# Group 3 by the DMA crossbar, in the one buffer that the later groups share

## The chip, the cores and the metric

The kernel runs on one core of a Trainium2 chip. The metric is device time in microseconds, the median of the runs of one kernel. The core has TensorE (PE, matmuls and their weight loads), VectorE (DVE), ScalarE (ACT) and GpSimd (POOL), and SyncE (SP), which here only issues DMAs. POOL issues the loads that convert from float32 to bfloat16. SP issues the stores of the result and the transposing DMAs through the crossbar. Each engine works through its own instructions in program order; semaphores hold one back until its inputs are there and its output buffer is free.

## The reference, cut to what matters

A sliding-window attention with four sink tokens feeds a SwiGLU block with three weight matrices.

```python
batch, n_heads, seq, head_dim = (4, 8, 768, 64)
n_sink, window = (4, 128)
scores = scale * np.matmul(q, k.transpose(0, 1, 3, 2))
keep = is_sink | in_window                 # 128 keys back, and keys 0 to 3
a = softmax(np.where(keep, scores, -1e9))
attn_out = np.matmul(a, v)                 # (4, 8, 768, 64)

x = attn_out.transpose(0, 2, 1, 3).reshape(3072, 512)
g, val = x @ w_gate, x @ w_val             # 512 -> 1536
out = (g * sigmoid(g) * val) @ w_out       # 1536 -> 512, float32
```

## The kernel before

The 3072 tokens of the attention are cut into 12 groups of 256, three to a batch. Group g is worked on in steps: its keys and queries are loaded with tokens in the partitions (`load_nat`), transposed so that the head's elements lie in the partitions, multiplied to scores (`step_S`), exponentiated, multiplied with the values (`step_PV`), normalised, and turned into columns of `xT` for the SwiGLU block (`step_X`). The SwiGLU block takes 8 blocks of tokens; `gate` does two projections, `down` the last one. The attention steps of later groups are woven between the `gate` and `down` steps of earlier blocks, so that TensorE always has matmuls at hand.

There are two ways to transpose keys and queries. `step_TN` lets TensorE do it into PSUM, and ACT or DVE copy the result out. `xbar` lets the DMA do it, from SBUF to SBUF, with four instructions from SP.

```python
rowp = pool("rowp", 3)     # three buffers, at first for staging, later for two groups
natp = pool("natp", 1)     # one buffer
...
def load_nat(g):
    b, c = divmod(g, GC)
    x = (natp if g > 3 else rowp).tile(
        [P, 2, 2, DM], BF16, tag="nat" if g > 3 else "rows", name="nat")
    for i, src in ((0, k), (1, q)):
        for j in range(2):
            t0 = c * 256 + j * P
            nc.gpsimd.dma_start(
                x[:, i, j].rearrange("p (h d) -> p h d", d=D),
                src[b, :, t0:t0 + P].rearrange("h p d -> p h d"))
    nats[g] = x

def load_v(g):
    b, c = divmod(g, GC)
    va = vpool.tile([P, 2, H, VS], BF16, tag=f"va{g}", name="va")   # a buffer per group
    nc.vector.memset(va[:, :, :, D:D + 1], 1.0)
    for j in range(2):
        ...
        nc.gpsimd.dma_start(va[:, j, :, 0:D], ...)
...
def step_TN(g, i, j, evict="av"):
    ...
    for p in range(NP2):
        nc.tensor.transpose(pt[:, p], nats[g][:, i, j, p * P:(p + 1) * P], ident)
    ...
    if evict[i] == "a":
        nc.scalar.copy(out=dst, in_=pt)
    else:
        nc.vector.tensor_copy(out=dst, in_=pt)

def xbar(g):
    ...
    for j in range(2):
        for i in range(2):
            t0 = c * 256 + j * P
            nc.sync.dma_start_transpose(
                (kTs, qTs)[i][b][:, :, t0:t0 + P], nats[g][:, i, j])
...
def step_X(g, j, evict="v"):
    ...
    if g not in PEX:                      # PEX = (0, 1, 2, 4)
        def sp():
            nc.sync.dma_start_transpose(xTs[tb][:, :, off:off + P], xns[g, j])
        later.append(sp)
        return
    ...
...
def down(tb, ts, attn, last=False):
    ...
        nc.scalar.activation(ot, po, AF.Copy, scale=0.5)
        nc.sync.dma_start(out[r0:r0 + P, lo:hi], ot)
...
flush()
load_nat(3)
load_v(3)
...
def NV(g):
    return L(A(load_nat, g), A(load_v, g))

# slot number -> attention steps woven into that gate or down step;
# slots 0 to 17 are gates of blocks 0 to 2, slots 18 to 23 their down steps
weave(us, slots(
    ...
    (11, [NV(4)]), ((14, 14, 15, 15), TN(3, "aa")),
    (15, [A(xbar, 4)]), (15, [NV(5)]), (19, [A(xbar, 5)]), (19, [NV(6)]),
    (23, [A(xbar, 6)]), (23, [NV(7)]),
    ((17, 18), Ss(3)), (18, [A(step_ks, 1)]), (18, [A(step_vsb, 1)]),
    ((19, 19, 19, 20), PVs(3)), (20, Xs(3)),
    ((19, 20), Ss(4)), (19, [K(4)]),
    ((21, 21, 22, 22), PVs(4)), (22, Xs(4))))
...
# block 3 (groups 3 and 4): gates, then down steps, with groups 5 and 6 woven in
weave(gates(3) + downs(3), slots(
    (2, [A(xbar, 7)]), (2, [NV(8)]),
    (5, [A(step_ks, 2), A(step_vsb, 2)]), *pair(5, 6),
    (15, [A(xbar, 8)]), (15, [NV(9)])))
```

A tile is given its buffer when it is asked for, and the first DMA into a buffer waits until all uses of the tile that held it before are done. So the load of group 5 into the single `nat` buffer waits for the four transposes of group 4 that read it, and so on to group 11.

Of the kernel before, what the change touches and what calls it, by code (L numbers as in the profile page):

```python
# [8 lines left out]
BF16 = mybir.dt.bfloat16  # L9
# [5 lines left out]
def kernel(  # L15
# [13 lines left out]
    P = 128  # L29
# [3 lines left out]
    DM = moe_w_gate.shape[0]  # L33
# [7 lines left out]
    NG = B * GC  # L41
# [11 lines left out]
    def pool(name, bufs, psum=False):  # L53
        if psum:
            return ctx.enter_context(
                tc.tile_pool(name=name, bufs=bufs, space=bass.MemoryType.PSUM))
        return ctx.enter_context(tc.tile_pool(name=name, bufs=bufs))
# [3 lines left out]
    rowp = pool("rowp", 3)  # L61
    natp = pool("natp", 1)
# [15 lines left out]
    def bank(shape, dtype, name):  # L78
        return psum.tile(shape, dtype, tag="b", name=name)


    rows, nats, vas = {}, {}, {}
# [20 lines left out]

    def load_nat(g):
        b, c = divmod(g, GC)
        x = (natp if g > 3 else rowp).tile(
            [P, 2, 2, DM], BF16, tag="nat" if g > 3 else "rows", name="nat")
        for i, src in ((0, k), (1, q)):
            for j in range(2):
                t0 = c * 256 + j * P  # L110
# [7 lines that stand above are left out]
        va = vpool.tile([P, 2, H, VS], BF16, tag=f"va{g}", name="va")  # L118
# [4 lines that stand above are left out]
                va[:, j, :, 0:D], v[b, :, t0:t0 + P].rearrange("h p d -> p h d"))  # L123
        vas[g] = va
# [71 lines left out]
    load_gate(2)  # L196
    nc.gpsimd.tensor_copy(out=vcf[64:128], in_=vcf[0:64])
    load_nat(2)
    load_gate(3)
    load_v(2)  # L200
# [18 lines left out]
    def new_T(b):  # L219
        if b not in kTs:  # L220
            kTs[b] = kqtp.tile([P, NP2, S], BF16, tag="kT", name="kT")
            qTs[b] = kqtp.tile([P, NP2, S], BF16, tag="qT", name="qT")
# [17 lines left out]
        else:  # L240
            nc.vector.tensor_copy(out=dst, in_=pt)

    def step_TN(g, i, j, evict="av"):

        b, c = divmod(g, GC)
        new_T(b)
        pt = bank([P, NP2, P], BF16, "pn")
        for p in range(NP2):
            nc.tensor.transpose(pt[:, p], nats[g][:, i, j, p * P:(p + 1) * P], ident)  # L249
        t0 = c * 256 + j * P  # L250
        dst = (kTs, qTs)[i][b][:, :, t0:t0 + P]
        if evict[i] == "a":
            nc.scalar.copy(out=dst, in_=pt)
        else:
            nc.vector.tensor_copy(out=dst, in_=pt)
# [213 lines left out]
    def gates(tb):  # L469
        return [(gate, tb, f) for f in range(0, DFC, 512 // SIZES[tb])]  # L470
# [4 lines left out]
    def A(fn, *a):  # L475
        return lambda: fn(*a)

    def TN(g, evict="av"):
        return [A(step_TN, g, i, j, evict) for j in range(2) for i in range(2)]

    def Ss(g):
        return [A(step_S, g, p2) for p2 in range(2)]
# [116 lines left out]
    later[:0] = masks1  # L599
    flush()  # L600
    load_nat(3)
    load_v(3)

    g0, g1, g2 = gates(0), gates(1), gates(2)
    us = [g0[0], g0[1], g0[2], g1[0], g1[1],
# [3 lines left out]
    def L(*fs):  # L609
        def f():  # L610
            for x in fs:
                x()
        return f

    def NV(g):
        return L(A(load_nat, g), A(load_v, g))

    weave(us, slots(
        (0, [K(1)]), (1, PVs(1)[:2] + [A(step_PV, 1, 0, 1, "a"), A(step_PV, 1, 1, 1, "a"), flush]),
        (2, [A(step_X, 1, 0, "a"), A(step_X, 1, 1, "a")]),  # L620
        ((4, 4, 5, 5), TN(2)), ((6, 7), Ss(2)), (6, [K(2)]),
        ((8, 8), PVs(2)[:2]), (9, [A(step_PV, 2, 0, 1, "a"), A(step_PV, 2, 1, 1, "a")]),
        ((10, 11), [A(step_X, 2, 0, "a"), A(step_X, 2, 1, "a")]),
        (11, [NV(4)]), ((14, 14, 15, 15), TN(3, "aa")),
        (15, [A(xbar, 4)]), (15, [NV(5)]), (19, [A(xbar, 5)]), (19, [NV(6)]),
        (23, [A(xbar, 6)]), (23, [NV(7)]),
        ((17, 18), Ss(3)), (18, [A(step_ks, 1)]), (18, [A(step_vsb, 1)]),
        ((19, 19, 19, 20), PVs(3)), (20, Xs(3)),
# [58 lines left out]
```

The softmax here doesn't subtract the row's maximum and nothing guards it: scores larger than these inputs give would overflow.

## Time and profile before

| | |
|---|---|
| median of 3 runs | 240.88 us (240.53 to 240.91) |
| span of the profiled run | 239.5 us |
| mean granted TensorE clock | 0.998 |
| PE busy | 232.2 us, 97% of the span |
| DVE busy | 158.6 us, 66% |
| ACT busy | 114.6 us, 48% |
| POOL busy (almost all of it issuing loads) | 73.2 us, 31% |
| share of the chain that ended last: PE | 84% |
| bytes read from HBM | 28.34 MB |
| written to HBM | 6.29 MB |

Busy time of the DMA-issuing instructions is the time to issue; a transfer lands later, and the profile gives the time from issue to landing for POOL's loads. The end of SP's transposing DMAs shows only in who waits for them. A row of the timeline has the start, the time covered, the engine, the line of the kernel, the operation with output and inputs, the count, and in brackets the idle time just before it and what ended it. "SPq" is SyncE's queue.

### The profile page before, as it was taken

How to read it: one execution, taken by the hardware profiler on the slowest of the kernel's cores; microseconds unless marked ns; L12 is line 12 of the kernel's file. 1: busy time of each engine (PE TensorE's matmuls, PEld its weight loads, DVE VectorE, ACT ScalarE, POOL GpSimd, SP SyncE). 2: the span in 40 equal slices, each digit the busy share in tenths (PEclk: the TensorE clock that was granted, in tenths of full speed). 3: DMA queues.
4: the chain of work that ended last, by engine and by line, in shares of the span. 5: the costliest groups of instructions: out<-in, count | busy, mean ns of one | idle time of the engine just before them, and what ended most of it. 6: DMA issues, size and time to landing. Idle time of an engine off the chain costs nothing.

```text
span 239.5 us, 4998 instructions
## 1 busy us (share of the span) xinstructions
PE 232.2 (97%) x1952; PEld 133.4 (56%) x1952; DVE 158.6 (66%) x336; ACT 114.6 (48%) x237; POOL 73.2 (31%) x94
## 2 busy tenths in 40 slices
PE   8998999999999999999999999999999999999994
PEld 5766978895454444444444454445454445488443
DVE  4799679678742898950798981588961598877000
ACT  3896385556552845512745611556611662332112
POOL 8985874712508043260080700071000000000000
PEclk9999999999999999999999999999999999999999
DMA  8999999993999999799699984699504200200122
GB/s 138 172 179 175 183 200 204 154 127 69 151 174 167 147 133 140 104 118 211 114 101 134 118 46 136 118 112 145 66 0 145 77 0 3 44 0 3 65 112 88
DMA packets 107591, 27.36 MB, mean 114 GB/s; under 512 B 94640, under 2 KB 104624, under 8 KB 107568
## 3 DMA queue, kind: packets, MB, share of 16 engines
q0 software_dynamic: 76640, 13.90, 75.7%
q1 hardware_dynamic: 30400, 12.89, 27.9%
q8 instruction: 15, 0.25, 0.4%
q10 hardware_dynamic: 528, 0.26, 0.4%
q14 instruction: 8, 0.07, 0.1%
HBM read 28.34 MB, written 6.29 MB: 145 GB/s over the span
## 4 chain that ended last, share of the span: by engine, by line
PE 84%; POOL 5%; DMA 4%; DVE 3%; issue 1%; ACT 1%; POOLq 0%; DVEq 0%; ACTq 0%
PE pd L458 26%; PE pv L427 24%; PE pg L427 24%; DMA wv<-in_moe_w_val_dram 4%; PE s L296 4%; PE o L359 4%; POOL va L122 1%; POOL rows L100 1%; DVE u L440 1%; PE pn L249 1%; POOL x L183 1%; POOL wg L133 1%; DVE ht L441 1%; POOL wv L133 1%; PE pk L324 1%
## 5 line engine op out<-in xcount | busy, mean ns | idle before, releaser
L427 PE MATMUL pv<-xT,wv 128*128 128x256 bf16 (+1 forms) x384 | 74.3, 326 | 1.1 <-DMA wv<-in_moe_w_val_dram 0.7
L427 PE MATMUL pg<-xT,wg 128*128 128x256 bf16 (+1 forms) x384 | 74.2, 326 | 0.9 <-DVE u L440 0.5
L434 ACT ACTIVATE th<-pg 128x512 f32<-128x512 f32 x72 | 43.5, 604 | 62.6 <-PE pg L427 62.1
L440 DVE SCALAR_TENSOR_TENSOR u<-th,pg 128x512 bf16<-128x512 f32 x72 | 49.2, 683 | 35.7 <-ACT th L434 35.7
L458 PE MATMUL pd<-wo,ht 128*128 128x512 bf16 (+1 forms) x300 | 66.2, 371 | 0.0
L441 DVE TENSOR_TENSOR ht<-u,pv 128x512 bf16<-128x512 bf16 x72 | 49.5, 688 | 11.5 <-PE pv L427 5.1
L427 PEld LDWEIGHTS <-wg 128*128 128x128 bf16 x384 | 37.4, 98 | 26.7 <-issue 1.3
L427 PEld LDWEIGHTS <-wv 128*128 128x128 bf16 x384 | 34.3, 98 | 20.5 <-issue 1.6
L303 ACT ACTIVATE e<-s 128x512 bf16<-128x512 f32 (+1 forms) x88 | 42.7, 582 | 3.9 <-PE s L296 3.9
L458 PEld LDWEIGHTS <-ht 128*128 128x128 bf16 x300 | 28.1, 98 | 28.7 <-issue 0.5
L111 POOL DMA_DIRECT2D nat<-in_k_dram x20 | 17.6, 884 | 79.6 <-DMA qT<-nat 68.5
L462 ACT ACTIVATE ot<-pd 128x512 f32<-128x512 f32 (+1 forms) x25 | 14.6, 583 | 48.4 <-PE pd L458 48.4
L308 DVE TENSOR_TENSOR e<-e,mask 128x1024 bf16<-128x1024 bf16 (+1 forms) x44 | 26.9, 649 | 3.6 <-ACT e L303 3.6
L122 POOL DMA_DIRECT2D va<-in_v_dram x24 | 21.5, 918 | 5.2 <-DMA wo<-in_moe_w_out_dram 2.5
L359 PEld LDWEIGHTS <-e 128*128 128x128 bf16 x352 | 15.4, 98 | 8.3 <-issue 0.3
L373 DVE TENSOR_TENSOR xn<-o,rcp 128x256 bf16<-128x256 f32 x44 | 18.7, 425 | 1.5
L111 POOL DMA_DIRECT2D nat<-in_q_dram x20 | 17.7, 897 | 1.8 <-DMA wg<-in_moe_w_gate_dram 1.2
L359 PE MATMUL o<-va,e 128*128 128x65 bf16 x352 | 17.5, 193 | 0.2 <-DMA va<-in_v_dram 0.2
L296 PE MATMUL s<-qT,kT 64*128 64x128 bf16 (+1 forms) x240 | 13.1, 237 | 0.0
L367 DVE RECIPROCAL rcp<-o 128x4 f32<-128x4 f32 x48 | 8.2, 175 | 5.6 <-PE o L359 5.4
L296 PEld LDWEIGHTS <-kT 64*128 64x128 bf16 x240 | 7.7, 94 | 7.3 <-issue 6.8
L133 POOL DMA_DIRECT2D wv<-in_moe_w_val_dram x6 | 4.8, 803 | 0.5 <-DMA wv<-in_moe_w_val_dram 0.5
(66 smaller groups left out, 84.0 us busy)
## 6 DMA issues: line engine op xcount, KB each, us to landing
out_dram<-ot SPq DMA_DIRECT2D x23, 256.0 KB
va<-in_v_dram POOLq DMA_DIRECT2D x24, 128.0 KB, 6.2
nat<-in_k_dram POOLq DMA_DIRECT2D x20, 128.0 KB, 4.0
nat<-in_q_dram POOLq DMA_DIRECT2D x20, 128.0 KB, 5.6
wg<-in_moe_w_gate_dram POOLq DMA_DIRECT2D x6, 256.0 KB, 8.0
wv<-in_moe_w_val_dram POOLq DMA_DIRECT2D x6, 256.0 KB, 8.5
wo<-in_moe_w_out_dram POOLq DMA_DIRECT2D x4, 384.0 KB, 11.1
st<-in_q_dram ACTq DMA_DIRECT2D x1, 256.0 KB
```

The source lines that it names most:

```text
L111: nc.gpsimd.dma_start(x[:, i, j].rearrange("p (h d) -> p h d", d=D), src[b, :, t0:t0 + P].rearrange("h p d -> p h d"))
L122: nc.gpsimd.dma_start(va[:, j, :, 0:D], v[b, :, t0:t0 + P].rearrange("h p d -> p h d"))
L296: nc.tensor.matmul(pss[2 * pp + h][:, col:col + n], kTs[b][r, p, kk:kk + P], qTs[b][r, p, qq:qq + n], start=True, stop=True)
L303: nc.scalar.activation(e_t[g][:, h0 + h, lo:512], pss[2 * pp + h][:, lo:512], AF.Exp, scale=scale)
L308: nc.vector.tensor_tensor(e, e, m[:, :, lo:512].broadcast_to([P, 2, 512 - lo]), op=ALU.mult)
L359: nc.tensor.matmul(o, l, r, start=(c == 0 and i == 0), stop=(i == len(mms) - 1), skip_group_check=True)
L373: nc.vector.tensor_tensor(xn, po[:, :, 0:D], rcp.broadcast_to([P, 4, D]), op=ALU.mult)
L427: nc.tensor.matmul(ps[:, i * n:(i + 1) * n], ws[fi][:, c, fo * P:(fo + 1) * P], x[:, c], start=(c == 0), stop=(c == DMC - 1))
L434: nc.scalar.activation(th, pg, AF.Tanh, scale=0.5)
L440: nc.vector.scalar_tensor_tensor(u, th, 1.0, pg, op0=ALU.add, op1=ALU.mult)
L441: nc.vector.tensor_tensor(hts[tb][:, f:f + two].rearrange("p a n -> p (a n)"), u, pv, op=ALU.mult)
L458: nc.tensor.matmul(po, hts[tb][:, f, ts * P:(ts + 1) * P], wos[f // n][:, f % n, lo:hi], start=(f == 0), stop=(f == DFC - 1))
```

## The change

Group 3's keys and queries are no longer transposed by TensorE out of a `rows` buffer; they go into the single `nat` buffer and are transposed by the crossbar, as those of the groups after it are. As the load of group 4's keys and queries then has to wait until group 3's have left that buffer, and would hold up all that POOL issues behind it, the values are moved ahead of it: group 4's values are loaded right after group 3's, and then group g + 1's values follow group g's keys and queries. It is meant to free TensorE of 16 transposes and ScalarE of 4 copies. The parameter that said which engine copies is dropped, as only group 2 uses `step_TN` now, with its default.

```diff
     def load_nat(g):
         b, c = divmod(g, GC)
-        x = (natp if g > 3 else rowp).tile(
-            [P, 2, 2, DM], BF16, tag="nat" if g > 3 else "rows", name="nat")
+        x = (natp if g > 2 else rowp).tile(
+            [P, 2, 2, DM], BF16, tag="nat" if g > 2 else "rows", name="nat")
...
-    def step_TN(g, i, j, evict="av"):
+    def step_TN(g, i, j):
...
-        if evict[i] == "a":
+        if i == 0:
             nc.scalar.copy(out=dst, in_=pt)
         else:
             nc.vector.tensor_copy(out=dst, in_=pt)
...
     flush()
     load_nat(3)
     load_v(3)
+    load_v(4)
...
     def NV(g):
-        return L(A(load_nat, g), A(load_v, g))
+        return L(A(load_nat, g), A(load_v, g + 1)) if g + 1 < NG else A(load_nat, g)
...
-        (11, [NV(4)]), ((14, 14, 15, 15), TN(3, "aa")),
+        (11, [A(xbar, 3)]), (11, [NV(4)]),
         (15, [A(xbar, 4)]), (15, [NV(5)]), (19, [A(xbar, 5)]), (19, [NV(6)]),
         (23, [A(xbar, 6)]), (23, [NV(7)]),
```

More of the change, by code (lines that the diff above doesn't have):

```diff
@@ L476, in A, with TN @@
         return lambda: fn(*a)
-    def TN(g, evict="av"):
-        return [A(step_TN, g, i, j, evict) for j in range(2) for i in range(2)]
+    def TN(g):
+        return [A(step_TN, g, i, j) for j in range(2) for i in range(2)]
     def Ss(g):
```

## The prediction, made before the run

> **What bounds the kernel now.** I read the page's busy row first, then the chain of work that ended last, then the list of who waited for whom, then the timelines of SyncE's queue, of GpSimd and of TensorE where the change lies (42 to 80 us), and the times from issue to landing of single loads. Busy row and chain:
>
> ```profile
> PE 232.2 (97%) x1952; PEld 133.4 (56%) x1952; DVE 158.6 (66%) x336; ACT 114.6 (48%) x237; POOL 73.2 (31%) x94
> ...
> PE 84%; POOL 5%; DMA 4%; DVE 3%; issue 1%; ACT 1%; POOLq 0%; DVEq 0%; ACTq 0%
> ```
>
> TensorE bounds it: 97% busy, and after about 23 us the chain hardly leaves it. Taking work from TensorE shortens the time by that work; any wait that TensorE gets lengthens it by that wait. What stands in the way is shown by the wait list:
>
> ```profile
> POOL nat L111 <- DMA qT<-nat: 68.5, 6, 20.7
> ```
>
> GpSimd waits 68.5 us in six waits for transposes of queries to leave the single buffer before it may load the next group. That costs nothing today, but it is a chain of its own (load, transpose, release, load), and the change puts one more group at its head. Its pace, from the timelines of SyncE and GpSimd:
>
> ```profile
> 50.24 1.29 SPq L263 DMA_TRANSPOSE kT<-nat  x1
> 51.98 1.76 SPq L263 DMA_TRANSPOSE qT<-nat  x1
> 53.83 1.22 SPq L263 DMA_TRANSPOSE kT<-nat  x1
> 55.14 1.22 SPq L263 DMA_TRANSPOSE qT<-nat  x1
> ...
> 67.37 2.00 SPq L263 DMA_TRANSPOSE qT<-nat  x1
> 69.46 0.53 SPq L463 DMA_DIRECT2D out_dram<-ot  x1
> 70.09 2.53 SPq L392 DMA_TRANSPOSE xT<-xn  x2
> ```
>
> ```profile
> 42.19 0.87 POOL L111 DMA_DIRECT2D nat<-in_k_dram  x1 [0.60 <-DMA wo<-in_moe_w_out_dram]
> ...
> 58.12 1.75 POOL L111 DMA_DIRECT2D nat<-in_k_dram  x2 [9.40 <-DMA qT<-nat]
> ...
> 71.79 1.76 POOL L111 DMA_DIRECT2D nat<-in_k_dram  x2 [8.42 <-DMA qT<-nat]
> ```
>
> Group 4 is loaded from 42.19 us, with no wait for a buffer, since it is the first in it. Its last transpose is issued at 55.14, and the buffer is free at 58.12 (2.98 us later). Group 5 takes the buffer from 58.12 to 71.79 (13.7 us). The page's digits of DMA share stand at 9 up to about 54 us: weights, then groups 3 and 4, drain one behind the other. TensorE at the three places that matter:
>
> ```profile
> 48.84 0.61 PE L249 MATMUL pn<-ident,nat 128*128 128x128 bf16 x8
> 49.29 1.04 PE L427 MATMUL pv<-xT,wv 128*128 128x256 bf16 x8
> ...
> 62.05 0.62 PE L296 MATMUL s<-qT,kT 64*128 64x128 bf16 x12
> ...
> 76.60 1.03 PE L427 MATMUL pg<-xT,wg 128*128 128x512 bf16 x4
> ```
>
> The first pair is half of group 3's transposes by TensorE, the third row group 4's first scores, the last row the first matmul of block 3. None of them waits for a DMA today: group 4's transposed queries are there 4 us before 62.05.
>
> **What the Trainium skill says.** "Perfetto Trace Analysis", section "DMA Instruction — HWDGE (DVE, Sync)", says that the profiled window of such a DMA is its issue and not the movement of its data. The trace agrees: the transpose issued at 55.14 ends its window at 56.36, and the buffer is free only at 58.12. So I count from issue to release. "DMA: Bandwidth & Descriptors", section "Issuing engines are not separate DMA queues", says that DMAs of all issuing engines run on the same 16 DMA engines and interleave. The trace agrees with sharing: the transpose that was issued while loads were still landing took 1.76 us instead of 1.22, and group 6, loaded beside three stores of 256 KB, held the buffer 15.1 us (71.79 to 86.91) against 11.7 us of group 9 (119.45 to 131.19). "TensorE: Matmul & The Clock Gate", section "What's actually happening", says that an idle window of about 3.4 us halves TensorE's clock. No run here shows it, the granted clock is 0.998; it matters to the upper end of the range.
>
> **The change, part by part.**
> Removed from TensorE: two times 8 transposes. From 48.84 to 49.29 and from 51.04 to 51.48 they take 0.45 and 0.44 us, together 0.89 us, on the path that sets the end. So -0.9 us.
> Removed from ACT: four copies of 580 to 606 ns, 2.4 us. ACT is 48% busy and idles before its next activation for want of TensorE (62.1 us in the wait list), so this is worth 0.
> Added: four transposing DMAs on SyncE, which has nothing else to issue from about 5.3 to 50 us. Worth 0 by themselves.
> Moved: group 4's values stand before its keys and queries. They take the places in the load queue that those had (two loads, issued at about 42.2 and 44.1). The values are no longer held up by the buffer, which prevents a worse result but wins nothing here: no value was late before (the only wait of a matmul for a value is one of 0.2 us).
> Moved, and this is the point: group 4's keys and queries now wait for the buffer. Step by step:
> 1. Group 3's load. Its four pieces are issued at 32.72, 33.79, 35.10 and 36.44, as before, and land 12.0, 11.9, 11.6 and 11.1 us later, at 44.7, 45.7, 46.7 and 47.5.
> 2. Its transposes go out in order keys, queries, keys, queries: 44.7, then 46.7 when the first queries land, then one after the other. With one prolonged issue of 1.76 beside the loads still draining: 48.5, then 49.8. Released 2.98 us after that: 52.8. The scores of group 3 are wanted at 55.07 - 0.9 = 54.2; that just holds.
> 3. Group 4's load begins at 52.8 instead of 42.19. From there to the release I take group 9's 11.7 us and not group 5's 13.7, because no store can get in front of or between these transposes in SyncE's queue. So group 4 is there at 64.5.
> 4. TensorE arrives at its scores at 62.05 - 0.9 = 61.15. It waits 64.5 - 61.15 = 3.35 us. All later work shifts by 3.35 - 0.9 = +2.45 us.
> 5. Group 5: loaded at 64.5, between 11.7 and 13.7 us, say 12.5: free at 77.0, its last transpose issued some 3.3 us before that, at 73.7. Behind it in SyncE's queue stand one store (0.5 us) and group 3's two columns of xT (1.3 us apart): 75.4 and 76.7 instead of 70.09 and 71.4. They land about 2.8 us after issue, at 79.5. TensorE wants them for block 3 at 76.60 + 2.45 = 79.05. A second wait of about 0.45 us.
> 6. Group 5's scores are wanted at 77.56 + 2.9 = 80.5 and are there at 77.0. Group 6 is loaded at 77.0, beside three stores as before, so 15.1 us: there at 92.1, wanted at 90.51 + 2.9 = 93.4. It holds by 1.3 us. From group 7 on the trace has slack: 7 is released at about 100 and wanted after 113. The delay is absorbed and no more is added.
> Sum: -0.9 + 3.35 + 0.45 = +2.9 us; 240.9 + 2.9 = 243.8 us.
>
> **The rivals.**
> First, the load chain holds and only TensorE's 0.9 us show: 240.0 us. For it: group 4's queries were ready 4 us before they were wanted, and group 3's buffer could be released faster than I think. Against it: the load starts 10.6 us later (42.19 to 52.8), it lands quicker by some 4.5 us as the queue is empty by then (8.0 us from issue to landing of its first piece before, 3.3 us for group 5), and of the remaining 6 us the slack covers only 4, less 0.9 as TensorE comes sooner.
> Second, the chain runs slower than I think: each cycle 13.7 us or more. Then group 4 comes at 66.5, group 5 at 80.2, the columns of xT at 82.7 against 81.0 wanted, and group 6 at 95.3 against 97. That is about +6.2 us, 247 us. For it: groups 5 and 6 took 13.7 and 15.1. Against it: stores contended there, and a late chain meets fewer of them.
> Third, the idle stretch of over 3 us makes TensorE's clock drop and adds one or two microseconds. Against it: a stall of 3.35 us hardly contains a whole window.
> A fourth, that ACT bounds something and its copies count, is refuted by its 62.1 us of waiting for TensorE.
>
> **Range and chances.** The centre is 243.8 us. The first rival bounds it below (240.0), but it needs both cycles to be 3 us shorter than any that the trace shows, so the low end is 241.8. The second rival gives 247.0 as the high end. The 2% limit above is 245.7: reached if the first two cycles together take about 2 us longer than I assume, 0.18. Faster by over 2% would need 4.8 us from a change that takes 0.9 us off TensorE: 0.02. Within 2%: 0.80.
>
> **What would show it.** In the changed kernel's timeline SyncE should issue group 3's transposes from 44.7 to about 49.8, GpSimd should start group 4's keys near 52.8 after a wait for "qT<-nat", and TensorE should show idle time of 3 to 3.5 us before the scores of group 4 with DMA qT or kT as releaser; that releaser should appear in the wait list of PE or its weight loads, where it is absent now. The two xT transposes should be issued near 75 to 77 us, with a small wait of the first pg matmul of block 3. After block 3's start no new wait should show. The prediction is wrong if group 4's first scores start before 62 us, if group 3's scores wait for their own transposes by more than a microsecond, or if a wait for DMA appears at group 6 or later.

## The result, and the profile after

The change makes the kernel slower: 246.92 us median against 240.91 us, a ratio of 1.0251 (95% interval 1.0217 to 1.0284). The prediction said 243.8 us: the direction is right, the growth forecast is half of the measured one (2.9 us against 6.0). The page of the changed kernel: busy row, granted clock in 40 slices, and the chain of work that ended last.

```profile
PE 233.9 (95%) x1936; PEld 133.0 (54%) x1936; DVE 158.2 (64%) x336; ACT 112.8 (46%) x233; POOL 73.2 (30%) x94
...
PEclk9999999999799999999999999999999999999999
...
PE 66%; DMA 20%; POOL 6%; SPq 2%; issue 2%; DVE 1%; ACT 1%; POOLq 0%; DVEq 0%
```

TensorE has 16 instructions fewer (1936 against 1952) and yet 1.7 us more of busy time, most of it from a stretch in which its clock was down (the 7). DMA has gone from 4% to 20% of the chain. Who TensorE waited for (total, times, longest):

```profile
PE pg L427 <- DMA xT<-xn: 4.2, 2, 2.9
PE s L296 <- DMA qT<-nat: 2.6, 2, 1.8
```

Both lines are new. The timelines of SyncE's queue, of GpSimd and of TensorE (start, time covered, engine, line, operation, count, idle time before and its releaser):

```profile
48.63 1.22 SPq L263 DMA_TRANSPOSE qT<-nat  x1
...
61.18 1.22 SPq L263 DMA_TRANSPOSE qT<-nat  x1
...
75.02 1.22 SPq L263 DMA_TRANSPOSE qT<-nat  x1
76.33 0.53 SPq L463 DMA_DIRECT2D out_dram<-ot  x1
76.96 2.55 SPq L392 DMA_TRANSPOSE xT<-xn  x2
79.60 1.54 SPq L463 DMA_DIRECT2D out_dram<-ot  x3
```

```profile
52.74 1.75 POOL L111 DMA_DIRECT2D nat<-in_k_dram  x2 [8.08 <-DMA qT<-nat]
...
64.71 1.76 POOL L111 DMA_DIRECT2D nat<-in_k_dram  x2 [6.71 <-issue]
...
78.01 1.76 POOL L111 DMA_DIRECT2D nat<-in_k_dram  x2 [8.04 <-DMA qT<-nat]
```

```profile
62.73 0.23 PE L296 MATMUL s<-qT,kT 64*128 64x128 bf16 x2 [1.84 <-DMA qT<-nat]
63.71 0.56 PE L296 MATMUL s<-qT,kT 64*128 64x256 bf16 x10 [0.75 <-DMA qT<-nat]
...
76.62 3.40 PE L458 MATMUL pd<-wo,ht 128*128 128x512 bf16 x15
82.97 1.02 PE L427 MATMUL pg<-xT,wg 128*128 128x512 bf16 x4 [2.95 <-DMA xT<-xn]
...
120.96 1.04 PE L427 MATMUL pg<-xT,wg 128*128 128x512 bf16 x4 [1.25 <-DMA xT<-xn]
```

The buffer goes to group 4 at 52.74, to group 5 at 64.71 and to group 6 at 78.01, where before group 4 was loaded from 42.19, group 5 from 58.12 and group 6 from 71.79. TensorE waits in three places: for group 4's scores until 63.71, for group 3's columns of xT, which block 3 needs, until 82.97, and for group 6's columns, which block 4 needs, until 120.96. Between the first two its clock is halved once; the windows view (stretch, length, busy time and count of PE, PEld, DVE, ACT, POOL, then the granted clock, DMA share and GB/s):

```profile
61.50:64.80 3.30, 1.32 (x22) 0.71 (x23) 0.00 (x0) 0.73 (x2) 0.09 (x1) 1.00 0.85 185
64.87:68.28 3.41, 3.41 (x16) 1.50 (x15) 1.99 (x4) 1.92 (x5) 3.41 (x5) 0.50 0.84 54
```

To see where the time came from, I set the start of the same matmul in both traces side by side; the difference, after less before, steps like this:

| matmul | before, us | after, us | difference | step |
|---|---|---|---|---|
| a pg before group 3's transposes | 47.97 | 47.63 | -0.34 | start of the kernel |
| first pg after the transposes | 52.36 | 51.12 | -1.24 | -0.90: 16 transposes gone |
| 22nd pd, after group 4's first scores | 62.60 | 64.20 | +1.60 | +2.84: wait for group 4 |
| 37th pd | 67.08 | 70.34 | +3.26 | +1.66: half clock |
| first pg of block 3 | 76.60 | 82.97 | +6.37 | +3.11: wait for group 3's xT |
| first pg of block 4 | 112.85 | 120.96 | +8.11 | +0.32 within block 3, +1.42: wait for xT again |
| last pd | 235.82 | 243.43 | +7.61 | -0.50 from block 4 on |

The half clock runs from 64.87 to 68.28, so it lies between the 22nd and the 37th pd. The profiled run took 248.64 us, 1.7 above the median, so in a median run the steps are smaller together; the kinds of steps are what the experiments below test.

One more thing stands in the trace. Group 3's last transpose has landed at 52.19 (the trace records the landing of SyncE's transfers too, though no view prints it). Group 4's load is issued at 52.74, and its first data move about 1.5 us later. The busy share of the DMA engines between 50 and 64 us, in tenths, in slices of 0.35 us:

```profile
DMA  9999600000001999999999999999999999999439
```

From about 52 to 54 us the engines stand idle, while TensorE will later wait for just this load.

### The profile page after: what moved, and what is told of

It is laid out like the page before. It is cut to its first block, busy times and chain, and to the rows that moved or that the text cites. A ratio compares the mean times of both kernels' runs of the same rounds, so it can differ in the third digit from the quotient of the medians.

```text
span 246.8 us, 4974 instructions
## 1 busy us (share of the span) xinstructions
PE 233.9 (95%) x1936; PEld 133.0 (54%) x1936; DVE 158.2 (64%) x336; ACT 112.8 (46%) x233; POOL 73.2 (30%) x94
## 4 chain that ended last, share of the span: by engine, by line
PE 66%; DMA 20%; POOL 6%; SPq 2%; issue 2%; DVE 1%; ACT 1%; POOLq 0%; DVEq 0%
PE pd L458 21%; PE pv L427 19%; PE pg L427 18%; DMA nat<-in_q_dram 7%; DMA xT<-xn 4%; DMA wv<-in_moe_w_val_dram 4%; DMA wg<-in_moe_w_gate_dram 3%; PE o L359 3%; PE s L296 3%; DMA qT<-nat 2%; SPq L263 2%; POOL va L122 2%; POOL wg L133 1%; POOL rows L100 1%; POOL nat L111 1%
## 5 line engine op out<-in xcount | busy, mean ns | idle before, releaser
L458 PE MATMUL pd<-wo,ht 128*128 128x512 bf16 (+1 forms) x300 | 67.7, 376 | 0.0
L296 PEld LDWEIGHTS <-kT 64*128 64x128 bf16 x240 | 7.8, 94 | 10.5 <-issue 7.5
```

The costliest lines, as they stand in the source:

```text
L296: nc.tensor.matmul(pss[2 * pp + h][:, col:col + n], kTs[b][r, p, kk:kk + P], qTs[b][r, p, qq:qq + n], start=True, stop=True)
L458: nc.tensor.matmul(po, hts[tb][:, f, ts * P:(ts + 1) * P], wos[f // n][:, f % n, lo:hi], start=(f == 0), stop=(f == DFC - 1))
```

## The experiments

All ratios are to the kernel before on the same chip, with 95% intervals; "us" is the median. My first theory was that of the prediction: group 4 waits for the one buffer. Its rival was that four more transposes, beside loads and in SyncE's queue, cost by themselves.

**Without the shared buffer, twice.** Group 3 by the crossbar, but out of its rows buffer:

```diff
--- before
-        (11, [NV(4)]), ((14, 14, 15, 15), TN(3, "aa")),
+        (11, [A(xbar, 3)]), (11, [NV(4)]),
```

> The kernel before with group 3 transposed by the crossbar, but out of its own rows buffer, loads in the old order: the change without the shared buffer. If the delay comes from group 4 waiting for the one buffer, nothing waits here and only TensorE's 16 transposes show: 240.9 - 0.9 = 240.0 us, group 4 loaded from about 42 us, clock never at 0.5 before the end. If the crossbar itself is the cost (four more transposes beside the weights' loads, SyncE's queue), a good part of the 6 us stays: 243 us or more.

Measured: 245.51 us, ratio 1.0190 (1.0153 to 1.0226). And the changed kernel with two buffers:

```diff
--- after
-    natp = pool("natp", 1)
+    natp = pool("natp", 2)
```

> The changed kernel with two buffers for keys and queries instead of one, all else as changed. If the single buffer is the cause, the wait before group 4's scores, the half clock and the wait for xT before blocks 3 and 4 all go: 240.0 us, like the run with the rows buffer, perhaps 0.5 us either way as loads come earlier and meet other stores. If the order of the loads (values ahead) is what delays, it stays above 243 us.

Measured: 245.33 us, 1.0185 (1.0139 to 1.0230). My theory is at best part of the cause: taking away the wait for the buffer brings back only about a quarter of the loss. TensorE of the run with the rows buffer:

```profile
53.62 1.04 PE L427 MATMUL pg<-xT,wg 128*128 128x256 bf16 x8
58.56 0.82 PE L296 MATMUL s<-qT,kT 64*128 64x256 bf16 x8 [3.90 <-DMA qT<-nat]
```

The same wait, 3.9 us, now stands one group earlier: at group 3's own scores. Group 3's last transpose was issued at 49.50, no later than in the changed kernel by more than a microsecond (48.63), but there it had landed by 52.19, and here only by 58.43. The difference is that here group 4's loads follow and land until 59.3, while in the changed kernel the wait for the buffer keeps them away. What the two queues moved between 48 and 57 us in the run with the rows buffer (q0 the loads, q1 SyncE's queue; packets, MB, and the time that the packets took as a share of 16 engines' span):

```profile
q0 software_dynamic: 4769, 0.60, 199.6%
q1 hardware_dynamic: 2667, 0.65, 74.9%
```

About half of the bytes are those of SyncE's queue. So the new theory: transposes and loads share the DMA engines and draw each other out, and the shared buffer only decides which group pays.

**What the transposes do to others.** The kernel before, TensorE still transposing group 3, plus four transposes of it into a tile that nobody reads (work added, none left out):

```diff
--- before
+    def xbar_spare(g):
+        for j in range(2):
+            for i in range(2):
+                nc.sync.dma_start_transpose(
+                    spare[:, i, :, j * P:(j + 1) * P], nats[g][:, i, j])
...
-        (11, [NV(4)]), ((14, 14, 15, 15), TN(3, "aa")),
+        (11, [A(xbar_spare, 3)]), (11, [NV(4)]), ((14, 14, 15, 15), TN(3, "aa")),
```

> The kernel before, unchanged in its results, plus four crossbar transposes of group 3's keys and queries into a tile that nobody reads; TensorE still transposes group 3 itself. It measures what four more transposes beside draining loads cost the rest. If transposes beside loads slow both down (the new theory, from the runs without the shared buffer), group 4's buffer is released near 62 us instead of 58.1 and the group's loads land up to 4 us later; as the scores of group 4 are wanted at 62.05, the time itself grows little: 241 to 242.5 us. If transposes are harmless to others and the delay lay in group 3's own dependency alone, release stays at 58.1 and the time at 240.9.

Measured: 243.07 us, 1.0093 (1.0058 to 1.0127). Group 5's load starts at 61.18 us instead of 58.12: four transposes on which nothing depends put the chain back by 3.1 us. The time is above what I expected, since the delay comes out again as 2.5 us of waiting for xT at block 3. The same with plain copies of the same bytes in place of the transposes:

```diff
--- the run before this one
-                nc.sync.dma_start_transpose(
-                    spare[:, i, :, j * P:(j + 1) * P], nats[g][:, i, j])
+                nc.sync.dma_start(
+                    spare[:, i, :, j * P:(j + 1) * P],
+                    nats[g][:, i, j].rearrange("p (a n) -> p a n", a=NP2))
```

> As the run with four spare crossbar transposes, but the four are plain copies of the same bytes from SyncE's queue into the same spare tile, in pieces of 256 bytes as well. If the slowdown is plain sharing of the 16 DMA engines, the loads are held up as much as by the transposes: group 5's load starts near 61.2 us instead of 58.1, time 242 to 243 us. If it is peculiar to crossbar transposes beside loads, the copies cost less than a microsecond: group 5's load before 59.5 us, time 240.8 to 241.3 us.

Measured: 242.04 us, 1.0040 (1.0025 to 1.0054); group 5's load starts at 60.41. Between the two expectations: 2.3 of the 3.1 us come with plain copies as well, so they are not peculiar to the crossbar; 0.8 us are left to it. The loads themselves are drawn out. Group 4's two loads of values, the last ones to drain, in the kernel before, beside the four transposes and beside the four copies (the last figure is us from issue to landing):

```profile
va<-in_v_dram POOLq DMA_DIRECT2D x2, 128.0 KB, 6.3
...
va<-in_v_dram POOLq DMA_DIRECT2D x2, 128.0 KB, 11.5
...
va<-in_v_dram POOLq DMA_DIRECT2D x2, 128.0 KB, 10.5
```

And so are the four transfers: the copies land 6.5 to 8.7 us after their issue, the transposes 7.3 to 9.1. How much of the delay of group 5 comes from this sharing, and how much from group 4's transposes standing behind the four in SyncE's queue, these two runs do not separate. The times differ by half a per cent: the wait for xT at block 3 is 0.7 us here and 2.5 us with the transposes.

**Group 3 earlier.** If time beside the loads is missing, an earlier load may find it:

```diff
--- group 3 out of the rows buffer (first run above)
     load_gate(5)
+    load_nat(3)
     for i in range(4):
         load_out(i)
...
-    load_nat(3)
     load_v(3)
```

> Group 3 by the crossbar out of its rows buffer, and its keys and queries loaded ahead of the four pieces of the output weights instead of behind them. If what was missing is time for group 3's transposes beside the draining loads, they now start near 37 us, are done by 48 and nothing waits at 54 us: 240.0 to 241 us. If group 4's transposes are then pushed past 61 us by the same traffic, a wait of 1 to 3 us appears there: 241 to 243. If the crossbar for a fourth group simply doesn't fit, it stays at 245.

Measured: 244.47 us, 1.0121 (1.0082 to 1.0160). The waits for group 3's and 4's scores are gone but for 0.5 us; a wait of 3.4 us for xT at block 3 stands in their place, with the half clock behind it (79.6 to 83.0 us). Slower than I expected, for a reason that I had not listed. Two of the six executions kept the clock (0.999 and 1.000) and took 242.09 and 242.28 us; the other four (0.992 to 0.993) took 244.44 to 244.65. The same shift of `load_nat(3)` in the changed kernel:

> The changed kernel (one buffer, values ahead) with group 3's keys and queries loaded ahead of the output weights. The chain through the buffer starts some 7 us earlier: group 3 released near 48, group 4 loaded from there behind the output weights and two groups of values, landed by 54, released near 60, wanted at 61.2: 240 to 241 us. If the chain's pace and not its start is what costs, 243 us or more.

Measured: 247.19 us, 1.0263 (1.0239 to 1.0287): nothing won. This is the clearest sight of the mechanism. SyncE's queue and GpSimd of this run:

```profile
41.02 3.21 SPq L264 DMA_TRANSPOSE qT<-nat  x1
```

```profile
51.82 1.75 POOL L111 DMA_DIRECT2D nat<-in_k_dram  x2 [11.35 <-DMA qT<-nat]
```

Group 3's last transpose is issued 7.6 us sooner than in the changed kernel, and the buffer is free only 0.9 us sooner. From issue of the last transpose to its landing, by how long loads went on landing beside it:

| kernel | last transpose issued | loads land until | landed | us |
|---|---|---|---|---|
| before (group 4) | 55.14 | 54.2 | 57.57 | 2.4 |
| changed (group 3) | 48.63 | 50.8 | 52.19 | 3.6 |
| rows buffer (group 3) | 49.50 | 59.3 | 58.43 | 8.9 |
| changed, loaded earlier (group 3) | 41.02 | 53.5 | 51.27 | 10.3 |

In each of the three runs with the single buffer GpSimd starts the next load 0.55 us after the landing. The transposes of the last two rows land about 1 and 2 us before the loads are through: they are drawn out by the loads, but do not wait for the last of them.

**The values.** The changed kernel with the values in the old order:

```diff
--- after
     load_v(3)
-    load_v(4)
...
-        return L(A(load_nat, g), A(load_v, g + 1)) if g + 1 < NG else A(load_nat, g)
+        return L(A(load_nat, g), A(load_v, g))
```

> The changed kernel with the values loaded in the old order, each group's behind its keys and queries. By the aim of the change group 4's values would come late: they are issued after group 4's keys and queries, about 56 us, land near 62, and are wanted for group 4's product at about 70 us, so I expect no harm. With two loads fewer beside group 3's transposes these end about 1 us sooner: 245.5 to 247 us. If the values are held up, a wait for values appears and it is slower than 248.

Measured: 244.71 us, 1.0153 (1.0124 to 1.0182), and no wait for values. The part of the change that was to protect it costs some 2 us of the 6. Where, the profile shows in part: group 4's load starts 0.7 us sooner here (52.02), but its transposes are through no sooner; the wait for xT at block 3 is 1.0 us instead of 2.95. And that part alone in the kernel before:

```diff
--- before
     load_v(3)
+    load_v(4)
...
-        return L(A(load_nat, g), A(load_v, g))
+        return L(A(load_nat, g), A(load_v, g + 1)) if g + 1 < NG else A(load_nat, g)
```

> The kernel before with only the values loaded one group ahead: group 3 stays with TensorE and its rows buffer. Group 4's keys and queries land two loads later, about 52 to 54 us, and group 5's by some 2 us later. If the values' place alone costs, 241.5 us or more, with a wait for xT at block 3; if it only costs together with the shared buffer, 240.9 within 0.4.

Measured: 242.06 us, 1.0026 (1.0003 to 1.0050): hardly above nothing, with waits for xT of 1.8 us in its profile, which is of its slowest execution (243.38 us). Its harm is mostly in company with group 3's transposes.

**The half clock.** Matmuls of zeros where TensorE waits for group 4:

```diff
--- after
         pss = [bank([P, 512], FP32, "s") for _ in range(4)]
+        if g == 4 and p2 == 0:
+            fill(24, pss[0])
```

> The changed kernel with 24 matmuls of zeros (2.6 us at full clock) put ahead of group 4's first scores, where TensorE waits anyway; they write a PSUM tile that the scores then overwrite. They should keep the clock at 1.0 between 64.9 and 68.3 us. If the lost clock adds to the time by itself, 246.9 - 1.4 = 245.5 us. If what follows is set by the chain load, transpose, SyncE's queue, xT, TensorE just arrives earlier at block 3 and waits longer there (2.95 us become about 4.3), and the time stays at 246.9 within 0.4.

Measured: 244.77 us, 1.0163 (1.0125 to 1.0201). The mean clock of its runs is 0.999 or 1.000, where those of the changed kernel had 0.984 to 0.993. Keeping the clock up is worth about 2 us. So the lost clock does add to the time; the second idea, that it would only lengthen the wait at block 3, is wrong: that wait is 1.7 us in this profile, not 4.3. The 2 us are not exact: among the changed kernel's own executions the time does not follow the clock (246.28 us at 0.984, 247.06 at 0.993).

**The columns of xT.** Group 3's by TensorE instead of SyncE's queue:

```diff
--- after
-    PEX = (0, 1, 2, 4)
+    PEX = (0, 1, 2, 3, 4)
```

> The changed kernel with group 3's columns of xT transposed by TensorE instead of SyncE's queue (8 transposes more on TensorE, 0.45 us, two copies on DVE). If they were late because they stand behind group 5's transposes in SyncE's queue, the wait before block 3 (2.95 us) goes: 246.9 - 3 + 0.5 + up to 0.5 of waiting for xn = 244.9 us. If block 3 is held by group 5's keys and queries as well, which are needed right after, little is won: 246 us or more.

Measured: 243.76 us, 1.0120 (1.0075 to 1.0165), a little better than expected; both waits for xT are gone, at block 4 as well. Of its four runs, two kept the clock (0.998 and 1.000) and took 242.59 and 243.19 us; two lost it for a while (0.993 and 0.991) and took 245.25 and 244.33. The half clock is worth about 1.9 us here too. Both edits together:

> The changed kernel with both: matmuls of zeros in the wait before group 4's scores, and group 3's columns of xT by TensorE. What is left is the first wait alone, less TensorE's saving: 240.9 - 0.9 + 3.1 + 0.5 (xT by TensorE) = 243.6 us less what xn lets overlap, so 242.5 to 243.6, the clock at 1.0 throughout, and no wait of TensorE for a DMA after 62 us. If the pieces don't add up, it stays with the run that has xT by TensorE only (243.8).

Measured: 243.77 us, 1.0107 (1.0063 to 1.0150), the clock at 0.999 to 1.000 in all four runs. That is just above the sum worked out and level with the run with xT alone, so the two gains do not add up. A likely reason, not shown, is that the matmuls of zeros cost time where the clock would have held: the two executions with xT alone that kept it took 242.59 and 243.19 us.

**Why xT came late.** In the changed kernel the first of group 3's two columns is issued at 76.96 and lands 2.4 us later; the second is issued at 78.28 and takes 4.6 us. Group 6's loads (from 78.01) and three stores (from 79.60) run beside the second. First the loads held until the columns have landed:

```diff
--- after
+    def behind_xT():
+        nc.gpsimd.tensor_copy(out=seen, in_=xTs[3][:, 0, 127:129])
...
-        (15, [A(xbar, 4)]), (15, [NV(5)]), (19, [A(xbar, 5)]), (19, [NV(6)]),
+        (15, [A(xbar, 4)]), (15, [NV(5)]), (19, [A(xbar, 5)]),
+        (21, [behind_xT, NV(6)]),
```

> The changed kernel, with group 6's loads held until group 3's columns of xT have landed (GpSimd first copies two elements of them). If the columns are late because group 6's loads run beside them, they land within 3 us of their issue, and the wait of block 3 falls from 2.95 to about 1 us; group 6 itself is loaded some 3 us later and may cost part of that again: 245 to 247 us. If the loads have nothing to do with it, the wait of block 3 stays near 2.9 us, and group 6's lateness adds to the time: 247 us or more.

Then the three stores put off, into a list that is issued after group 6's transposes:

```diff
--- after
-            nc.sync.dma_start(out[r0:r0 + P, lo:hi], ot)
+            if (tb, ts) in ((1, 0), (1, 1), (2, 0)):
+                held.append(store)          # store: the same dma_start
+            else:
+                store()
...
-        (2, [A(xbar, 7)]), (2, [NV(8)]),
+        (1, [let_go]), (2, [A(xbar, 7)]), (2, [NV(8)]),
```

> The changed kernel, with the three stores of 256 KB that follow group 3's columns of xT in SyncE's queue moved behind group 6's transposes. If these stores slow the columns, the wait of block 3 falls to about 1 us and the time to 245 us; if the loads of group 6 or the mere place in the queue do, the wait stays at 2.5 to 3 us and the time near 246.9, or a little less as group 6's loads land sooner.

Measured: 247.46 us, 1.0237 (1.0205 to 1.0270), and 247.03 us, 1.0210 (1.0147 to 1.0272). Ratios leave out executions more than 1.5% above the fastest of the same kernel: 252.19 us of the changed kernel, 251.35 of the first run here and 248.88 of the second, which is the one profiled. The times don't tell them apart, the first matmul of block 3 does; of the run with the loads held, and then of the one with the stores put off:

```profile
80.39 1.03 PE L427 MATMUL pg<-xT,wg 128*128 128x512 bf16 x4
```

```profile
84.50 1.02 PE L427 MATMUL pg<-xT,wg 128*128 128x512 bf16 x4 [3.27 <-DMA xT<-xn]
```

With the loads held, the second column lands 2.4 us after its issue and block 3 doesn't wait. With the stores put off, it takes 4.8 us and block 3 waits 3.3 us as before. The loads do it. Why the time gains nothing is shown in part: group 6 comes later and block 4 waits 1.8 us for its xT instead of 1.25, which is less than the 2.95 us won. The profile is of the fastest execution (246.24 us, clock 0.993); two others, at 247.22 and 247.70, had a clock of 0.986, and where they lost it no profile shows.

**A version that beats both, by little.** Group 3 out of the rows buffer, loaded early, and its xT by TensorE (the edits of three runs above together):

> Group 3 by the crossbar out of the rows buffer, loaded ahead of the output weights, and its columns of xT by TensorE. The run without the last of these had one wait left, 3.4 us for xT before block 3, with the half clock after it. If that is the last place where the added transposes bite, this lands at 240.0 to 240.8 us; if a wait for group 5's or 6's keys and queries takes its place, 242 or more.

Measured: 240.57 us, 0.9979 (0.9962 to 0.9996). TensorE finds groups 3 and 4 ready:

```profile
53.50 0.50 PE L297 MATMUL s<-qT,kT 64*128 64x256 bf16 x8
...
60.48 0.62 PE L297 MATMUL s<-qT,kT 64*128 64x128 bf16 x12
```

No wait of TensorE for a DMA above 0.5 us at a time is left. What remains is TensorE's 16 transposes less the 8 that xT takes, 0.45 us, and the median is 0.5 us lower. That the transposes win it is not shown: the kernel before with the earlier load alone was not run.

## Why the prediction was wrong in size

- "Added: four transposing DMAs on SyncE", "Worth 0 by themselves": the step that failed first. It looked at whether SyncE was free to issue and not at the DMA engines that move the data. Four spare transposes at this place cost 2.3 us (243.07 against 240.81 us).
- "Removed from TensorE", -0.9 us: right, 0.90 in the trace. ACT's copies worth nothing: no run speaks against it.
- Steps 1 to 4, the wait for group 4: right. Predicted: last transpose of group 3 at 49.8, group 4's load at 52.8, ready at 64.5, a wait of 3.35 us. Measured: 48.63, 52.74, 64.71, and 2.84 in the table above. That 52.8 was hit so well is luck: the transpose was issued 1.2 us sooner than said, and the load started 4.1 us after it and not 2.98, as loads still landed beside it.
- Third rival, "a stall of 3.35 us hardly contains a whole window": wrong. The clock was halved for 3.41 us right after it, worth 1.66 us in the trace and about 2 us by the run with matmuls of zeros. It had to be a term of the sum and was only a remark on the range.
- Step 5, "a second wait of about 0.45 us": the term that was mis-sized most, 2.95 us of waiting and 3.11 in the table. Group 5 took the buffer for 13.3 us and not 12.5, so the columns were issued at 76.96 and 78.28 and not at 75.4 and 76.7; and the second landed 4.6 us after issue and not 2.8, since group 6's loads ran beside it. A time like the 2.8 fits a stretch in which the loads have drained, as after 55.14 in the trace of before (2.4).
- Step 6, "from group 7 on the trace has slack" and "no more is added": right for keys and queries, wrong for xT. Block 4 waited 1.25 us for group 6's columns; holding group 6's scores ready by a margin was not the same as having its columns in time. With this the prediction's own sign of being wrong, a wait for DMA at group 6 or later, came true. I followed one chain and forgot that the same queue and the same loads carry another.
- "Moved: group 4's values ... wins nothing here": it costs about 2 us. Two loads more drain beside group 3's transposes and the chain starts 0.7 us later; the rest shows as a longer wait for xT.
- The reason as a whole, "group 4's keys and queries now wait for the buffer", describes the trace but is only part of the cause. With that wait taken away the ratio is still 1.019, as group 3's own scores then wait 3.9 us. What lacks is DMA time between about 44 and 62 us: the loads of groups 3 and 4 and now eight transposes instead of four want the same engines, and the buffer either lets them collide or, as here, holds the loads off while the engines idle. The second rival, a slower chain, gave 247 us, close to the result, but with group 4 at 66.5 us (64.7 measured) and without the half clock and block 4: its closeness is luck.

The sum was -0.9 + 3.35 + 0.45. In the trace these terms are -0.90, 2.84 and 3.11, and three more stand beside them: 1.66 for the clock, 1.74 up to block 4, and -0.84 from the start of the kernel and from block 4 on.

What stays open: what decides how the DMA engines are shared between SyncE's queue and the loads. Plain copies are drawn out nearly as much as transposes, so it is not peculiar to the crossbar.

## What to carry to other kernels

A transfer's time depends on the traffic beside it, so take it from a place with the same traffic. Before moving work from a full TensorE to DMA, look whether the DMA engines have room just then; in this kernel four transposes of 128 KB that nothing waited for cost 0.9%. And when a chain of loads shifts, follow every other transfer that shares its engines and its queue, down to the next block, and count a wait near 3 us as one that may cost the clock as well: here one of 1.84 and 0.75 us did, one of 3.4 us did in the run with group 3 loaded earlier, and the one of 2.95 us did not.

## What the runs showed of the hardware

- TensorE's clock was halved after a stretch that was not idle: from 61.5 to 64.8 us PE was busy for 1.32 of 3.30 us, and the clock stood at 0.50 from 64.87 to 68.28. The Trainium skill ("TensorE: Matmul & The Clock Gate", section "What's actually happening") speaks of an idle window of about 3.4 us. The halved stretch is that long (3.41 us); the stretch ahead of it was not idle throughout. Whether it happens depends on the run: with xT by TensorE it did in two runs of four.
- A transposing DMA of 128 KB landed 2.4 us after its issue with the loads drained, and 8.9 to 10.3 us with loads draining beside it.
- Four plain copies of 128 KB from SBUF to SBUF put the start of group 5's load back by 2.3 us, four crossbar transposes of the same bytes by 3.1 us. Loads that drained beside them took 10.5 and 11.5 us from issue to landing, against 6.3 without.
